# An attention and feed-forward kernel whose order of operations comes from deadlines: 141 recorded moves of the deadlines

## The chip, the cores and the metric

The kernel runs on one core of a Trainium2 chip. The metric is the time of one execution on the device in microseconds, from three runs of the kernel before. The engines are TensorE (PE; its weight loads are listed as PEld), VectorE (DVE), ScalarE (ACT), GpSimd (POOL) and SyncE (SP), which issues all transfers from and to memory.

## The reference

Attention of 8 batches and 8 heads, with keys and values averaged over 8 neighbours, and on its output a feed-forward layer of 512 to 2048 to 512 features:

```python
k_p = k.reshape(B, H, Sp, pool, D).mean(axis=3)          # B, H = 8, 8; S = 576, D = 64, pool = 8, Sp = 72
v_p = v.reshape(B, H, Sp, pool, D).mean(axis=3)
scores = scale * np.matmul(q, k_p.transpose(0, 1, 3, 2))
attn = softmax(scores)
x = np.matmul(attn, v_p) ...reshape(B * S, H * D)         # 4608 x 512
h = x @ w_in                                              # 512 x 2048
sp = np.maximum(h, 0.0) + np.log1p(np.exp(-np.abs(h)))
g = h * erf(sp)
return (g @ w_out).astype(np.float32)                     # 2048 x 512
```

## The kernel before

The 4608 tokens are nine chunks of 512. Attention makes the columns of x for a chunk (tiles att, in banks of PSUM): scores of up to 128 tokens (line 637), their maxima, differences, the exponential by way of a sigmoid, sums and scaling on VectorE, ScalarE and GpSimd (tiles m, s, z), transposes on TensorE (line 692), and the product with the values (lines 755, 756, 826). The feed-forward layer works on numbers that are split in a high and a low half, with three matmuls of 128x512 for each product (function `pairs`, line 826). A low half is the difference of line 446, which may run on VectorE or on GpSimd; a high half is line 434 (ScalarE) or 435 (GpSimd). Tiles h are the first GEMM, o the second, g the activated values between them, gl their halves; x and xr are the layer's inputs, w and ws weights and sums of weights.

Chunk 0 is computed plainly (stage 0). While this runs, the weights arrive in 64-bit words, are converted, and are written back to memory as halves. The other eight chunks go in pairs (stages 1 to 4), by a scheme with seven products instead of eight: function `quad` makes four tiles of h with seven products on four banks, and between the products VectorE adds what lies in a bank to a running sum (line 929). A second product onto a bank may start only when the addition that reads the first one is done. In stages 2 to 4 the second GEMM uses such a scheme too (function `seconds`, differences on line 992).

The activation of four tiles is two softplus operations of ScalarE for each pair (line 845), an error function for each pair (line 849), and a product on VectorE or GpSimd (lines 853, 856). Softplus and error function need different tables, and a change of table is an ACT_TABLE_LOAD. There are 8 banks of PSUM; a new tile waits until one is free.

Nothing of the order is written by hand. The kernel records operations with a deadline each, and the planner plays them through: method `once` starts, again and again, the operation that can start first on some engine, with costs per operation, limits on buffers and a price for a change of table, and its choice leans on the deadlines. Where an operation may run on two engines (`both`, `copy`, `out_of_bank`), `once` decides as well. The deadlines come from method `order`: eight passes, each with deadlines taken from the latest possible starts of the pass before; the best pass counts. Then the moves follow, of which the kernel before has none:

```python
for seed in MOVES:
    h = mix(seed)
    spread, reach = SPREAD[(h >> 20) % 3], REACH[(h >> 40) % 3]
    middle = -10000.0 + (mix(h ^ 0x1234567) >> 11) / 2.0 ** 53 * (SPAN + 10000.0)
    for i, t in enumerate(at):
        if abs(t - middle) < reach:
            g = mix(h + i)
            g = sum(float(g >> 16 * k & 65535) for k in range(4))
            at[i] = t + spread * ((g - 131070.0) / 37837.0)
```

Each seed stands for a middle, a reach (6, 20 or 60 us on the planner's scale) and a spread (0.3, 1 or 3 us): the deadlines within reach of the middle are shifted by random amounts. The operations are then played through once more with these deadlines, and written down in that order. Where the planner sees TensorE idle for over 1.2 us (in the first 57 us of its scale, for any time), it puts fillers into TensorE's queue, matmuls of constants onto the next free bank, 128x256 in bf16 (line 1127).

Of the kernel before, what the change touches and what calls it, by code (L numbers as in the profile page):

```python
# [41 lines left out]
BY_BLOCK = lambda ck: True  # L42
PASSES, UNIT = 8, 5100.0
SPREAD, REACH, SPAN = (300.0, 1000.0, 3000.0), (6e3, 20e3, 60e3), 860e3
MOVES = ()
T0, T0_STEP = -10.5, 1.5
VAL_R = 3.5
KEYS, KEYS_R, KEYS_S = -5.5, 0.5, -1.0
# [64 lines left out]
def mix(x):  # L113

    m = 2 ** 64 - 1
    x = x + 0x9E3779B97F4A7C15 & m
    x = (x ^ x >> 30) * 0xBF58476D1CE4E5B9 & m
    x = (x ^ x >> 27) * 0x94D049BB133111EB & m
    return x ^ x >> 31
# [33 lines left out]
class Program:  # L153
# [78 lines left out]
    def order(self, passes=PASSES):  # L232
# [13 lines left out]
        at = list(best[1])  # L246
        for seed in MOVES:
            h = mix(seed)
# [924 lines left out]
```

## Time and profile before

| | |
|---|---|
| time, median of 3 runs | 835.78 us (831.79 to 838.14) |
| the profiled execution's own time | 837.19 us |
| its span, first to last instruction | 835.4 us |
| mean granted clock of TensorE | 0.993 |
| TensorE busy | 811.6 us (97%) |
| VectorE, ScalarE, GpSimd busy | 696.5, 573.9, 445.2 us |
| read and written in memory | 167.84 and 49.28 MB |

Busy times are sums over the whole span, in which stages with different limits follow each other. Matmuls overlap in the record (one of 128x512 is listed with 381 ns), so that the time from one to the next is read from rows that hold many of them. The granted clock is the share of full speed that TensorE is given.

### The profile page before, as it was taken

Reading aid. Unit: us, or ns where it says so; the run is one execution under the profiler, and the core shown is the slowest. Engines: PE = TensorE matmul, PEld = TensorE weight load, DVE = VectorE, ACT = ScalarE, POOL = GpSimd, SP = SyncE. Lnnn points to the kernel's source line nnn. Section 1 sums busy time; section 2 is a strip of 40 time slices with the busy share of each in tenths; the row PEclk is TensorE's granted clock in tenths of the full one; section 3 lists DMA queues with packets and bytes.
Section 4 is the critical chain, followed back from the end, with each engine's and each line's share of the span. In section 5 each row is a group of like instructions: output and inputs, shape, how many; then the busy total and the mean of one; then the engine's idle time right before and its main releaser. Section 6 shows DMA issues by size and latency. Waiting matters only on the chain.

```text
span 835.4 us, 13512 instructions
## 1 busy us (share of the span) xinstructions
PE 811.6 (97%) x4091; PEld 703.4 (84%) x4091; DVE 696.5 (83%) x1235; ACT 573.9 (69%) x976; POOL 445.2 (53%) x441
## 2 busy tenths in 40 slices
PE   8998998999989989999999999999999999999998
PEld 7786887878878888888888888888878888888887
DVE  6976899887788999598988999978989995677972
ACT  5999876679974564477885544888955456999730
POOL 2884775568867871077657533363574311652330
PEclk9998999999999999999999999999999999999999
DMA  9889999799997899995486478943653689448641
GB/s 337 325 292 357 332 339 363 262 365 360 341 381 266 299 377 310 331 387 161 164 287 205 139 247 271 366 144 101 203 190 123 216 290 338 143 133 277 202 150 68
DMA packets 134695, 218.03 MB, mean 261 GB/s; under 512 B 17120, under 2 KB 49248, under 8 KB 134624
## 3 DMA queue, kind: packets, MB, share of 16 engines
q1 hardware_dynamic: 134624, 217.18, 75.6%
q8 instruction: 33, 0.54, 0.3%
q14 instruction: 38, 0.31, 0.1%
HBM read 167.84 MB, written 49.28 MB: 260 GB/s over the span
## 4 chain that ended last, share of the span: by engine, by line
PE 64%; DVE 6%; ACT 1%; issue 1%; DVEq 0%
PE o L826 31%; PE h L826 27%; PE att L637 3%; PE att L826 2%; PE att L692 1%; DVE s L684 1%; DVE gl L446 1%; PE att L756 1%; DVE e L708 1%; DVE vr L598 1%; DVE g L853 0%; DVE z L669 0%; ACT e L706 0%; DVE m L646 0%; ACT d L849 0%
## 5 line engine op out<-in xcount | busy, mean ns | idle before, releaser
L826 PE MATMUL o<-gl,w 128*128 128x512 f32 x1536 | 342.5, 381 | 4.7 <-DVE gl L446 4.2
L826 PEld LDWEIGHTS o<-gl,w 128*128 128x128 f32 x1536 | 287.2, 189 | 46.3 <-DVE gl L446 5.6
L826 PE MATMUL h<-x,w 128*128 128x512 f32 x1344 | 302.8, 385 | 3.9 <-DVE t L929 2.1
L826 PEld LDWEIGHTS h<-x,w 128*128 128x128 f32 x1344 | 255.4, 192 | 43.4 <-DVE t L929 3.0
L853 POOL TENSOR_TENSOR g<-d,g 128x512 f32<-128x512 f32 x76 | 98.9, 1318 | 132.6 <-ACT d L849 85.0
L434 ACT ACTIVATE gl<-g 128x512 fp32r<-128x512 f32 x177 | 102.7, 623 | 52.8 <-DVE g L992 27.5
L446 POOL TENSOR_TENSOR gl<-g,gl 128x512 fp32r<-128x512 f32 x63 | 90.7, 1445 | 77.9 <-ACT gl L434 73.4
L446 DVE TENSOR_TENSOR gl<-g,gl 128x512 fp32r<-128x512 f32 x145 | 114.3, 818 | 1.6 <-POOL gl L435 1.2
L929 DVE TENSOR_TENSOR g<-t,h 128x512 f32<-128x512 f32 x96 | 65.6, 685 | 27.8 <-PE h L826 26.7
L849 ACT ACTIVATE d<-d 128x1024 f32<-128x1024 f32 x72 | 74.1, 1053 | 0.5
L845 ACT ACT_TABLE_LOAD x48 | 61.6, 1283 | 14.5 <-PE h L826 13.2
L845 ACT ACTIVATE d<-g 128x512 f32<-128x512 f32 x103 | 59.1, 622 | 3.5 <-DVE g L929 3.4
L992 POOL TENSOR_TENSOR g<-g 128x512 f32<-128x512 f32 x40 | 53.4, 1338 | 11.5 <-DVE g L992 5.1
L849 ACT ACT_TABLE_LOAD x46 | 59.0, 1283 | 0.8
L929 DVE TENSOR_TENSOR t<-t,h 128x512 f32<-128x512 f32 x57 | 39.1, 686 | 22.1 <-PE h L826 18.1
L637 PE MATMUL att<-kbd,q 128*128 128x144 f32 (+1 forms) x320 | 46.8, 289 | 0.2 <-ACT kbd L587 0.2
L434 ACT ACTIVATE x<-xr 128x512 fp32r<-128x512 f32 (+2 forms) x53 | 28.7, 560 | 24.6 <-DVE xr L800 15.0
L637 PEld LDWEIGHTS att<-kbd,q 128*128 128x128 f32 (+1 forms) x320 | 41.6, 179 | 3.9 <-issue 0.7
L826 PE MATMUL h<-x,ws 128*128 128x512 f32 x192 | 44.1, 381 | 0.8 <-DVE x L446 0.5
L992 DVE TENSOR_TENSOR g<-g 128x512 f32<-128x512 f32 x56 | 42.9, 779 | 0.3
L646 DVE TENSOR_REDUCE m<-att 128x4 f32<-128x288 f32 (+1 forms) x80 | 34.3, 446 | 9.9 <-PE att L637 9.5
L826 PEld LDWEIGHTS h<-x,ws 128*128 128x128 f32 x192 | 35.9, 189 | 6.6 <-DVE x L446 0.9
(105 smaller groups left out, 1120.7 us busy)
## 6 DMA issues: line engine op xcount, KB each, us to landing
w<-ws SPq DMA_DIRECT2D x192, 256.0 KB, 4.8
w<-wo SPq DMA_DIRECT2D x136, 256.0 KB, 4.2
w<-wi SPq DMA_DIRECT2D x96, 256.0 KB, 5.1
ws<-ws SPq DMA_DIRECT2D x64, 256.0 KB, 4.7
v<-vl SPq DMA_DIRECT2D x48, 256.0 KB, 5.1
out<-f SPq DMA_DIRECT2D x35, 256.0 KB, 2.3
k<-kl SPq DMA_DIRECT2D x32, 256.0 KB, 5.2
q<-qa SPq DMA_DIRECT2D x32, 256.0 KB, 5.0
```

The costliest lines, as they stand in the source:

```text
L434: op("ACT", act(n), prio, lambda: nc.scalar.activation(dst(), src(), AF.Copy, scale=scale), *access, turn=turn, alt=("POOL", 0.833 * n + 1 ...
L446: both(True, dve(n), gps(n), prio + 0.1, lambda e: e.tensor_sub(lo(), src(), f32(hi())), reads + [hikey], [lokey])
L598: op("DVE", dve(4 * D), due + VALS_S, lambda mk=mk, sl=sl: nc.vector.scalar_tensor_tensor(vr.ap[:, :, sl], vs.ap[:, 0:NP, :], mk, f32(va.a ...
L637: nc.tensor.matmul(o, raw.ap[:, p, :T], kbd[:, p], start=(p % 2 == 0), stop=True, skip_group_check=True)
L646: op("DVE", dve(4 * SP), r + 0.4, lambda pv=pv, gs=gs: nc.vector.tensor_reduce(m.ap[:T, gs], pv(), AX.X, ALU.max), [ps], [(m, g)])
L684: both(ck < 3, dve(H * SP), gps(H * SP), r + 1.2, lambda e: e.tensor_mul(*[s.keys[:T].rearrange("t p (x k) -> t p x k", x=2)] * 2, z.ap[:T ...
L826: nc.tensor.matmul(o, u, v, start=first and q == 0, stop=last and q == 2, skip_group_check=True)
L845: nc.scalar.activation(y(k), hs[k][0].ap, AF.Softplus)
L849: op("ACT", act(1024), prio + 0.2, lambda k=k: nc.scalar.activation(ys[k].ap, ys[k].ap, AF.Erf), own[2 * k:2 * k + 2], own[2 * k:2 * k + 2 ...
L853: both(True, dve(512), gps(512), prio + 0.3, lambda e, k=k, h=h: e.tensor_mul(h.ap, y(k), h.ap), [own[k], h], [h])
L929: op("DVE", dve(512), prio, lambda: nc.vector.tensor_add(dst.ap, u.ap, o.ap), [u, o], [dst])
L992: both(True, dve(512), gps(512), prio, lambda e: e.tensor_sub(out.ap, u.ap, v.ap), [u, v], [out])
```

## The change

The table `MOVES` is filled with 141 seeds. They were found by a local search that played the whole order through for each trial. Nothing else is changed; lines below the table move by 13, so that line 826 is 839 in the changed kernel, 929 is 942, 446 is 459, 853 is 866.

```diff
-MOVES = ()
+MOVES = (
+    2000003, 2000010, 2000013, 2000026, 2000038, 2000052, 2000055, 2000062, 2000073, 2000099, 2000108,
...
+    2300967, 2328338, 2374855, 2378219, 2382978, 2438662, 2462926, 2495042,)
```

All five engines get another order. TensorE has 3876 rows before and 3812 after (180 fillers with a weight load each before, 148 after), VectorE 1216 and 1214, ScalarE 890 and 913, GpSimd 446 and 441, SyncE 815 both times. Table loads of ScalarE are 97 before and 87 after. Three places follow.

The first place is VectorE in stage 1, where the products of the quads meet the first matmuls of the second GEMM (some 226 to 235 us of the trace before). Tiles t are running sums of a quad, h its banks. Before:

```order
L929 TENSOR_TENSOR t_3006<-t_3000,h_2973 128x512
L446 TENSOR_TENSOR ws_3017<-sw_2921,ws_2986 128x512
L853 TENSOR_TENSOR g_2877<-d_2954,g_2877 128x512
L853 TENSOR_TENSOR g_2835<-d_2939,g_2835 128x512
L853 TENSOR_TENSOR g_2717<-d_2874,g_2717 128x512
L446 TENSOR_TENSOR gl_3045<-g_2472,gl_2997 128x512
L929 TENSOR_TENSOR t_3058<-t_3006,h_3034 128x512
L578 TENSOR_REDUCE vs_2925<-v_3003 128x64
L929 TENSOR_TENSOR g_3074<-t_3058,h_3049 128x512
L929 TENSOR_TENSOR g_3085<-t_3006,h_3034 128x512
```

And now, at the same place:

```order
L942 TENSOR_TENSOR t_2999<-t_2984,h_2976 128x512
L675 TENSOR_TENSOR s1_72<-att_2895,m_2965 128x2x144
L866 TENSOR_TENSOR g_2855<-d_2929,g_2855 128x512
L866 TENSOR_TENSOR g_2794<-d_2949,g_2794 128x512
L866 TENSOR_TENSOR g_2732<-d_2840,g_2732 128x512
L459 TENSOR_TENSOR gl_3043<-g_2333,gl_3025 128x512
L459 TENSOR_TENSOR gl_3056<-g_2562,gl_3036 128x512
L942 TENSOR_TENSOR t_3063<-t_2999,h_3029 128x512
L591 TENSOR_REDUCE vs_2917<-v_3011 128x64
L591 TENSOR_REDUCE vs_2917<-v_3058 128x64
L942 TENSOR_TENSOR g_3088<-t_3063,h_3049 128x512
L942 TENSOR_TENSOR g_3101<-t_2999,h_3029 128x512
```

Between the two additions into t there now stand two low halves (gl) instead of one and a difference of a softmax tile (s1) instead of a difference of weights (ws); the three products (g) stay. The same place on TensorE, from the last matmul of the first product onto the bank h_3034 to the first of the second. Before:

```order
L826 MATMUL h_3034<-x_2238,ws_3017 128x512
L826 MATMUL h_3049<-x_2108,ws_2952 128x512
L826 MATMUL h_3049<-x_2134,ws_2952 128x512
L826 MATMUL h_3049<-x_2108,ws_2969 128x512
L826 MATMUL h_3049<-x_2119,ws_2952 128x512
L826 MATMUL h_3049<-x_2140,ws_2952 128x512
L826 MATMUL h_3049<-x_2119,ws_2969 128x512
L826 MATMUL h_3034<-x_2288,w_2756 128x512
```

Now the bank is h_3029; the last six matmuls onto it stand seven to twelve rows ahead of this piece's third row:

```order
L839 MATMUL h_3049<-x_2147,ws_2903 128x512
L839 MATMUL h_3049<-x_2129,ws_2921 128x512
L839 MATMUL h_3049<-x_2118,ws_2903 128x512
L839 MATMUL h_3049<-x_2135,ws_2903 128x512
L839 MATMUL h_3049<-x_2118,ws_2921 128x512
L839 MATMUL o_2990<-gl_2608,w_3027 128x512
L839 MATMUL o_2990<-gl_2852,w_3027 128x512
L839 MATMUL o_2990<-gl_2608,w_3027 128x512
L839 MATMUL o_2994<-gl_2608,w_3027 128x512
L839 MATMUL o_2994<-gl_2852,w_3027 128x512
L839 MATMUL o_2994<-gl_2608,w_3027 128x512
L839 MATMUL h_3029<-x_2293,w_2821 128x512
```

Where six matmuls onto another bank stood between the two products, there are now these and six of the second GEMM.

The second place is ScalarE at the end of stage 0 (some 85 to 95 us of the trace before). Tiles d hold softplus and then its error function, cv, w0 and xr are other work. Before:

```order
L845 ACT_TABLE_LOAD
L845 ACTIVATE d_1230<-h_1121 128x512
L845 ACTIVATE d_1230<-h_1155 128x512
L849 ACT_TABLE_LOAD
L849 ACTIVATE d_1230<-d_1230 128x1024
L495 ACTIVATE cv_1262<-d_1143 128x512
L495 ACTIVATE cv_1275<-d_1153 128x512
L495 ACTIVATE cv_1279<-d_1173 128x512
L434 ACTIVATE w0_1289<-f0_1277 128x512
L440 COPY xr_1300<-att_1286 128x64
L667 ACTIVATE s3_74<-s3_74,cst_75 128x4x144
L845 ACT_TABLE_LOAD
```

And now:

```order
L858 ACT_TABLE_LOAD
L858 ACTIVATE d_1280<-h_1189 128x512
L858 ACTIVATE d_1280<-h_1123 128x512
L858 ACTIVATE d_1295<-h_1216 128x512
L858 ACTIVATE d_1295<-h_1251 128x512
L862 ACT_TABLE_LOAD
L862 ACTIVATE d_1280<-d_1280 128x1024
L862 ACTIVATE d_1295<-d_1295 128x1024
L608 ACTIVATE va_1359<-vs_520,cst_75 128x4x64 x2
```

Two pairs of softplus operations stand together, and then both error functions: two table loads for four tiles, where two tiles had two.

The third place is late in stage 1, where the second chunk's output begins (some 291 to 297 us of the trace before). There VectorE had, with gl_3842 the low half that the seventh group of matmuls onto the new banks uses:

```order
L446 TENSOR_TENSOR ws_3788<-sw_3675,ws_3742 128x512
L578 TENSOR_REDUCE vs_3800<-v_3181 128x64
L578 TENSOR_REDUCE vs_3800<-v_3231 128x64
L578 TENSOR_REDUCE vs_3800<-v_3255 128x64
L669 TENSOR_REDUCE z_3830<-s1_72 128x8
L674 RECIPROCAL z_3830<-z_3830 128x8
L446 TENSOR_TENSOR gl_3842<-g_2497,gl_3685 128x512
L578 TENSOR_REDUCE vs_3800<-v_3828 128x64
```

In the new order this half is gl_3791, on GpSimd:

```order
L554 TENSOR_TENSOR sw_3518<-sw_3518,sw_3491 128x256
L555 TENSOR_TENSOR sw_3722<-sw_3606 128x256
L556 TENSOR_TENSOR sw_3583<-sw_3482,sw_3518 128x256
L459 TENSOR_TENSOR ws_3741<-sw_3518,ws_3724 128x512
L459 TENSOR_TENSOR ws_3758<-sw_3583,ws_3743 128x512
L553 TENSOR_TENSOR sw_3776<-sw_3606,sw_3548 128x256
L459 TENSOR_TENSOR gl_3791<-g_2499,gl_3683 128x512
L554 TENSOR_TENSOR sw_3776<-sw_3776,sw_3606 128x256
L459 TENSOR_TENSOR gl_3822<-g_2475,gl_3701 128x512
```

The half has moved from VectorE, where sums of values (vs) and of a softmax tile (z) stood ahead, to GpSimd, where sums and differences of weights (sw, ws) stand ahead.

## Rows read from the trace of the kernel before

**Rows 1.** The page, part 1: busy us (share of the span) x instructions.

```profile
PE 811.6 (97%) x4091; PEld 703.4 (84%) x4091; DVE 696.5 (83%) x1235; ACT 573.9 (69%) x976; POOL 445.2 (53%) x441
```

**Rows 2.** The chain that ended last, 300 to 360 us: start, us, what.

```profile
317.64 25.90 PE o L826 x120
```

**Rows 3.** By stretch: busy us of PE, PEld, DVE, ACT, POOL; granted clock; DMA share, GB/s.

```profile
36.00:93.00 57.00, 53.26 (x254) 45.73 (x252) 41.05 (x77) 53.69 (x70) 39.98 (x45) 0.94 0.96 325
93.00:187.00 94.00, 90.10 (x455) 76.19 (x454) 84.39 (x146) 68.17 (x127) 61.70 (x71) 1.00 0.93 331
...
245.00:300.00 55.00, 52.84 (x283) 46.11 (x282) 49.39 (x98) 30.67 (x64) 45.46 (x49) 1.00 0.90 304
300.00:598.00 298.00, 296.85 (x1520) 260.85 (x1519) 263.44 (x492) 201.13 (x335) 149.31 (x138) 1.00 0.72 245
598.00:630.00 32.00, 29.56 (x155) 25.30 (x154) 28.89 (x56) 19.78 (x43) 19.87 (x20) 1.00 0.55 181
```

**Rows 4.** TensorE's waits: us in total, times, longest.

```profile
PE o L826 <- DVE gl L446: 4.2, 3, 2.2
PE att L1127 <- DMA cst<-cst: 2.7, 1, 2.7
PE att L692 <- DVE g L856: 2.3, 1, 2.3
...
PE h L826 <- DVE t L929: 2.1, 1, 2.1
```

**Rows 5.** TensorE's timeline at 204 us: start, us, line, tiles, count [idle before].

```profile
203.85 1.37 PE L1127 MATMUL h<-cst 128*128 128x256 bf16 x11
...
206.37 2.03 PE L1127 MATMUL h<-cst 128*128 128x256 bf16 x17
```

**Rows 6.** Busy us in two short stretches, columns as in rows 3.

```profile
66.00:74.00 8.00, 7.15 (x21) 5.58 (x20) 4.79 (x9) 7.63 (x12) 4.10 (x5) 0.57 1.04 343
233.00:238.00 5.00, 4.18 (x12) 3.44 (x13) 3.17 (x7) 0.91 (x2) 2.71 (x4) 0.66 1.05 396
```

**Rows 7.** Timeline at 62 to 68 us, ScalarE and TensorE.

```profile
63.81 2.00 ACT L849 ACTIVATE d<-d 128x1024 f32<-128x1024 f32 x2
...
65.73 0.43 PE L692 MATMUL att<-cst,s 64*128 64x64 f32 x4 [2.27 <-DVE g L856]
...
67.29 7.99 PE L826 MATMUL h<-x,w 128*128 128x512 f32 x22 [0.32 <-DVE g L856]
```

**Rows 8.** Timeline at 227 to 234 us, VectorE and TensorE.

```profile
227.01 4.49 DVE L853 TENSOR_TENSOR g<-d,g 128x512 f32<-128x512 f32 x3
...
231.42 1.75 DVE L446 TENSOR_TENSOR gl<-g,gl 128x512 fp32r<-128x512 f32 x1
...
233.82 4.51 PE L826 MATMUL h<-x,w 128*128 128x512 f32 x12 [2.11 <-DVE t L929]
```

**Rows 9.** ScalarE's timeline at 58 us: a table load and what follows.

```profile
58.28 1.28 ACT L845 ACT_TABLE_LOAD   x1
...
59.57 1.09 ACT L845 ACTIVATE d<-h 128x512 f32<-128x512 f32 x2
```

**Rows 10.** TensorE's waits from 75 to 125 us.

```profile
PE h L826 <- DVE g L856: 0.6, 1, 0.6
PE o L826 <- DVE g L856: 0.4, 1, 0.4
```

**Rows 11.** TensorE's timeline at 294 to 298 us.

```profile
296.31 1.99 PE L826 MATMUL o<-gl,w 128*128 128x512 f32 x8 [2.16 <-DVE gl L446]
```

**Rows 12.** The page, part 5: low halves on GpSimd and on VectorE.

```profile
L446 POOL TENSOR_TENSOR gl<-g,gl 128x512 fp32r<-128x512 f32 x63 | 90.7, 1445 | 77.9 <-ACT gl L434 73.4
L446 DVE TENSOR_TENSOR gl<-g,gl 128x512 fp32r<-128x512 f32 x145 | 114.3, 818 | 1.6 <-POOL gl L435 1.2
```

**Rows 13.** Timeline at 617 to 627 us, TensorE.

```profile
618.74 0.63 PE L692 MATMUL att<-cst,s 128*128 128x128 f32 x4 [1.03 <-DVE s L684]
...
627.05 3.29 PE L826 MATMUL o<-gl,w 128*128 128x512 f32 x14 [1.32 <-DVE gl L446]
```

11 rows, old and new, of the table MOVES are left out of this document.

## Prediction

> **What bounds the kernel now.** I read first the busy shares, then the stretches, then TensorE's waits, then the timeline at the longest of them. The busy shares name TensorE: 811.6 us of 835.4 [rows 1]. How long that work must take at the least is better seen in a stretch without any wait: 120 matmuls of 512 columns took 25.90 us there [rows 2], 0.216 us each, and nearly every matmul of the kernel is of this form. The stretches [rows 3] show where more than that is lost. From 300 to 598 us TensorE is busy 296.85 of 298 us: no order can win anything there. What can be won lies before 300 us, and a little at 598 to 630 us, and there other engines are close to their own limit: ScalarE with 53.69 of 57 us from 36 on, VectorE with 84.39 of 94 us from 93 on. TensorE's waits after the start add up to little: the three large groups behind the first transfer are 8.6 us [rows 4], all others some 8 us more. To these come 37 fillers after the start (matmuls without use that the planner sets where it expects a gap; two groups stand in [rows 5], 28 of the 37), and two stretches in which the granted clock falls, 0.57 on the mean from 66 to 74 us and 0.66 from 233 to 238 us [rows 6], to the lower of the two levels (1.2 GHz), each just behind a wait of TensorE of over 2 us. At that level 22 matmuls took 7.99 us [rows 7] where 22 x 0.216 = 4.75 us would do, a loss of 3.2 us; 12 matmuls took 4.51 us [rows 8] against 2.6, a loss of 1.9 us. So the whole that an order can win behind the start is about 17 (waits) + 37 x 0.11 = 4.1 (fillers) + 5.1 (clock) = 26 us.
>
> The sum is made against the profiled execution, 837.19 us, of which 835.4 are the span; the median of the three runs, 835.78, is 1.4 us below it, and the result is moved down by that.
>
> **The change, part by part.** No operation is added or taken away from the computation. What changes is the order on all five engines, on which of two engines an operation runs where the planner may choose, the number of table loads, and the number of fillers.
>
> Fillers. One of them is 0.11 us: 17 took 2.03 us and 11 took 1.37 us, six more in 0.66 us [rows 5]. Before there are 143 ahead of the first useful matmul of the first GEMM and 37 behind it; now 138 and 10. The ten stand in one group early in the same stage, and the groups of 11, 17 and 9 are gone. A filler stands in TensorE's queue and is always executed, so each one less is a gain if its gap is gone too: 32 x 0.11 = 3.5 us. If the gap stays and only its cover goes, the gain is nothing. I take all of it, since what stood around the two large groups was moved as well (next paragraphs).
>
> Table loads of ScalarE. Each takes 1.28 us [rows 9], and there are 97 before, 87 now. Up to the 16th softplus 14 become 12, up to the 32nd 26 become 22, because four softplus operations now more often stand together and then their two error functions. In the first of these stretches that is 2 x 1.28 = 2.6 us off an engine that is busy 94% of it. But TensorE follows ScalarE there at a few places only: its waits for a bank that a product of softplus and error function must free are 0.6 and 0.4 us [rows 10], and 2.27 us at 65.7 us [rows 7]. This last one I leave as it is: ScalarE's two error functions for four banks [rows 7] stand in the same place of the changed order, with one operation of 0.6 to 1 us less ahead of them. So of 2.6 us I count 1.0; the bounds are 0 and 2.6. In the Trainium skill, "ScalarE: Activation LUTs", section "What ACT_TABLE_LOAD costs", a switch is said to cost a load and a drain, some 2.66 us together. The next activation here starts 1.29 us after a load began [rows 9], so that no drain shows behind it; by the page the two loads would be 5.3 us and the sum lower by up to 2.7 us.
>
> The wait at 231.7 us. In a quad (four tiles made by seven products) the second product onto a bank must wait until VectorE has added up the first. Before, six matmuls (1.3 us) lie between the two, and VectorE had three products of 1.5 us each, a subtraction of 1.75 us and the addition ahead [rows 8]; TensorE stood still for 2.11 us, and the clock fell. Now twelve matmuls lie between (1.3 us more cover). VectorE's work between the two additions concerned is about the same: three products, two subtractions instead of one and a small one of a softmax tile, no weight difference. So the wait should fall from 2.1 to about 0.8 us, and a wait of that length stood nowhere before a drop in these rows: 1.3 + 1.9 = 3.2 us. Bounds: 0 if VectorE is as much later as TensorE, and 4.0.
>
> The wait at 294.2 us. TensorE waited 2.16 us for the low half of an operand, which VectorE made as the last of a chain without idle time [rows 11]. At the corresponding place of the new order GpSimd makes it, behind a row of weight sums. A half takes 1.445 us there and 0.818 on VectorE [rows 12]; GpSimd was busy 45.46 of 55 us in this stretch [rows 3], so it is not free either. I count half, 1.1 us; bounds -1 (GpSimd is later still) and 2.2. A rule of the Trainium skill speaks against this move ("SBUF — State Buffer", section "Who interferes with whom"): an operation of VectorE with both inputs in SBUF and one of GpSimd that reads SBUF exclude each other through a shared port. Rows agree as far as they go: VectorE's products took 1.5 us each beside a busy GpSimd [rows 8]. By it the halves moved would take back what they give, and this term would be 0.
>
> The waits at 617 and 625 us, 1.03 and 1.32 us [rows 13]. The first is for the scaling of a softmax tile. Now the two transposes that follow the last scores are those of tiles scaled long before (VectorE's rows 922 and 941, the last maxima being rows 955 and 956), and the remaining two stand behind 54 more matmuls, 11.7 us. The second wait is for a half on VectorE, which is as full as before (28.89 of 32 us). I count the first alone: 1.0; bounds 0 and 2.4.
>
> The start and the end are left: the same 45 fillers, and the last 339 matmuls stand as before. Loads from memory are reordered too (815 rows of SyncE both times); the one wait of TensorE for a transfer is the first, 2.7 us [rows 4], and I price this at nothing; a weight that comes late would cost up to such a wait, and one that comes earlier gains nothing, as none is waited for.
>
> The sum: 3.5 + 1.0 + 3.2 + 1.1 + 1.0 = 9.8 us. 837.2 - 9.8 = 827.4, less 1.4: **826 us**, 1.2% below the median.
>
> **Rivals.** (a) The waits move and don't go. VectorE is busy 88 to 90% in the four stretches shown from 93 us on [rows 3], so what is taken from one wait comes back at the next; only fillers count, and about 32 x 0.11: 835.8 - 3.5 = 832 us. For it: each of the shown waits hangs on a different instruction, and all of them are reordered. Against it: ScalarE's ten loads less and the longer distance in the quads are real relief. (b) The new order is slower. From 93 to 187 us VectorE is busy 90%. In the new order 328 of its rows lie ahead of the 32nd addition of the quads, before 322; at 696.5 us / 1235 = 0.56 us [rows 1] that is 3.4 us, and if VectorE is the bound there, TensorE waits for them in two or three pieces of over 2 us (together with what is waited there now). Each can bring a drop as behind 65.7 us: 3.4 + 3 x 3.2 - 3.5 = +9.5 us, 845 us. It decides if such a wait is over 2 us long. Against it: TensorE's waits in this stretch are short now, and of the three long ones (2.27, 2.11, 2.16 us) one had no drop behind it. (c) Almost all waits go: 835.8 - 26 = 810 us. For it: the planner sees fewer gaps of the size that it fills, one where there were three; against it: a wait at 65.7 us whose order did not change.
>
> **How the numbers follow.** Forecast 0.45, (a) 0.29, (b) 0.16, (c) 0.10. The forecast's own range is made of its bounds: all terms at their best 3.5 + 2.6 + 4.0 + 2.2 + 2.4 = 14.7 us (821), at their worst only part of the fillers and one late half, about 833. Some 1% (8.4 us) is what a measurement of this kernel can tell from no change, since its three runs are 6 us apart. 826 is just outside of it, so that about a fifth of the forecast's chance lies within: faster 0.36 + 0.10 = 0.46, within 1% 0.09 + 0.29 = 0.38, slower 0.16. The range from 813 to 841 us takes in the forecast, (a), half of (c) and little of (b).
>
> **What would show it.** In the profile after: TensorE's busy time down by some 3.5 us with 148 rows of the filler; 43 and 42 table loads at the two lines of the activation where 48 and 46 were; no wait of TensorE over 1 us, and no granted clock under 0.9, where the quads of the first stage meet the second GEMM (some 225 to 240 us); the wait at 65.7 us and the drop behind it still there. The prediction is wrong if the clock falls at a new place before 250 us, if VectorE's additions of the quads release TensorE more often than before, or if TensorE waits for a transfer.

## The result and the profile after

The changed kernel takes 824.09 us (median of 4 runs, 822.35 to 824.77), the kernel before 835.70 us beside it (4 runs, 831.79 to 838.14): ratio 0.9862, interval 0.9821 to 0.9903. The forecast was 826 us. Over all 81 executions of the kernel before that were made beside the experiments its median is 836.66 us. The profiled execution of the changed kernel took 822.35 us, span 820.5 us, with a mean granted clock of 1.000. Against the profiled execution of before that is 14.9 us of span, more than the medians show (11.6). Both are single executions, and that of before has two drops of the clock (mean granted clock 0.993, where the 81 have 0.989 to 0.999).

The page of the changed kernel, part 1, as in [rows 1]:

```profile
PE 801.7 (98%) x4059; PEld 697.5 (85%) x4059; DVE 695.4 (85%) x1224; ACT 568.9 (69%) x982; POOL 446.6 (54%) x436
```

Its stretches, columns as in [rows 3]:

```profile
36.00:93.00 57.00, 54.99 (x274) 47.13 (x273) 45.20 (x83) 54.92 (x74) 45.63 (x51) 1.00 0.94 331
93.00:187.00 94.00, 89.88 (x461) 77.53 (x460) 84.50 (x149) 70.25 (x130) 56.39 (x63) 1.00 1.00 353
187.00:245.00 58.00, 58.00 (x282) 50.56 (x281) 53.81 (x86) 52.96 (x67) 45.84 (x45) 1.00 0.99 350
245.00:300.00 55.00, 54.17 (x303) 47.67 (x302) 49.46 (x97) 31.75 (x75) 39.02 (x45) 1.00 0.90 317
```

The kernel before in the one of these stretches that [rows 3] leave out:

```profile
187.00:245.00 58.00, 55.89 (x270) 47.92 (x269) 44.62 (x69) 51.90 (x63) 44.80 (x44) 0.97 1.02 358
```

The clock is 1.00 in all four stretches, its upper level. TensorE stands still nowhere from 187 to 245 us, and VectorE does 53.81 us of work there where it did 44.62, although its work over the whole span is the same (695.4 and 696.5 us). TensorE's longest waits, as in [rows 4] (line 705 is 692 in the kernel before, 768 is 755):

```profile
PE att L705 <- DVE s L697: 3.0, 4, 1.3
PE att L1140 <- DMA cst<-cst: 2.6, 1, 2.6
PE att L768 <- DVE s L675: 2.2, 1, 2.2
PE h L839 <- DVE t L942: 1.6, 2, 0.9
PE att L708 <- POOL bb L693: 1.4, 1, 1.4
PE att L705 <- DVE g L869: 1.1, 1, 1.1
```

Of the three waits of over 2 us that the kernel before has behind the start none is left; one of 2.2 us, at 120 us, is new. The waits for low halves are down from 4.2 us to 0.2. Around 62 to 66 us, as in [rows 7]:

```profile
61.93 2.01 ACT L862 ACTIVATE d<-d 128x1024 f32<-128x1024 f32 x2
...
63.77 0.24 PE L708 MATMUL att<-cst,bb 64*64 64x64 f32 x1 [0.20 <-DVE g L869]
...
65.09 0.46 PE L705 MATMUL att<-cst,s 64*128 64x64 f32 x4 [1.09 <-DVE g L869]
...
65.78 8.01 PE L839 MATMUL h<-x,w 128*128 128x512 f32 x36 [0.23 <-DVE g L869]
```

ScalarE's two error functions begin 1.9 us earlier than before, TensorE waits 1.5 us in three pieces, and 36 matmuls behind them take 8.01 us (0.22 each), where before 22 took 7.99. At the quads, as in [rows 8]:

```profile
226.07 1.46 PE L839 MATMUL o<-gl,w 128*128 128x512 f32 x6
226.39 0.68 DVE L942 TENSOR_TENSOR t<-t,h 128x512 f32<-128x512 f32 x1
...
227.36 2.75 PE L839 MATMUL h<-x,w 128*128 128x512 f32 x12
```

VectorE's addition ends at 227.07, 0.29 us ahead of the second product. Table loads are 43 and 42, as the order said, 1.283 us each:

```profile
L858 ACT ACT_TABLE_LOAD x43 | 55.2, 1283 | 22.7 <-PE h L839 12.7
...
L862 ACT ACT_TABLE_LOAD x42 | 53.9, 1283 | 0.7
```

Since waits move, where the time went is best read from TensorE's own progress: when it starts its 1st, 140th, 460th, 930th and last (3133rd) matmul of 512 columns. The starts were counted in the traces; the table gives the time between them in us, for both kernels and five of the experiments below (each is one profiled execution).

| | to 1st | to 140th | to 460th | to 930th | to last |
|---|---|---|---|---|---|
| before | 36.3 | 38.1 | 95.6 | 127.2 | 533.5 |
| changed | 35.7 | 34.2 | 95.7 | 117.9 | 532.3 |
| e5: moves of deadlines under 110 us | 36.1 | 34.3 | 95.2 | 129.2 | 534.6 |
| e6: moves from 110 us | 35.8 | 37.7 | 104.7 | 117.9 | 530.9 |
| e7: moves under 330 us | 36.3 | 34.2 | 97.7 | 118.1 | 533.9 |
| e8: moves from 330 us | 36.3 | 36.4 | 95.2 | 129.1 | 534.8 |
| e4: before with four edits by hand | 35.7 | 37.3 | 95.7 | 122.3 | 536.2 |

Nearly all of the gain lies in two pieces: 3.9 us up to the 140th matmul (about 70 us), and 9.2 us between the 460th and the 930th (166 to 284 us). The second piece can be added up from the two traces: before, it holds 28 fillers (3.0 us), 5.1 us of TensorE's waits and the drop behind the wait at 231.7 us (1.9 us, as the prediction reckoned it); in the changed kernel it holds no filler, 1.4 us of waits and no drop. That is 8.6 of the 9.2 us. The experiments ask what made all three go.

### The profile page after: what moved, and what is told of

Same layout as the page of the kernel before. It is cut to its first block, busy times and chain, and to the rows that moved or that the text cites. A ratio compares the mean times of both kernels' runs of the same rounds, so it can differ in the third digit from the quotient of the medians.

```text
span 820.5 us, 13391 instructions
## 1 busy us (share of the span) xinstructions
PE 801.7 (98%) x4059; PEld 697.5 (85%) x4059; DVE 695.4 (85%) x1224; ACT 568.9 (69%) x982; POOL 446.6 (54%) x436
## 4 chain that ended last, share of the span: by engine, by line
PE 47%; DVE 2%; DMA 1%; ACT 0%; issue 0%; DVEq 0%; SPq 0%; ACTq 0%
PE o L839 24%; PE h L839 19%; PE att L650 1%; PE att L839 1%; PE att L705 1%; DVE g L1005 1%; DVE gl L459 1%; DMA w<-ws 1%; DVE s L697 0%; PE att L769 0%; PE att L708 0%; ACT gl L447 0%; DVE etb L737 0%; DVE e L721 0%; ACT e L719 0%
## 5 line engine op out<-in xcount | busy, mean ns | idle before, releaser
L839 PE MATMUL h<-x,w 128*128 128x512 f32 x1344 | 297.5, 380 | 2.3 <-DVE t L942 1.6
L839 PEld LDWEIGHTS h<-x,w 128*128 128x128 f32 x1344 | 252.4, 189 | 39.6 <-DVE t L942 2.4
L459 DVE TENSOR_TENSOR gl<-g,gl 128x512 fp32r<-128x512 f32 x149 | 116.8, 815 | 1.8 <-POOL gl L448 0.9
L459 POOL TENSOR_TENSOR gl<-g,gl 128x512 fp32r<-128x512 f32 x59 | 85.5, 1454 | 53.4 <-ACT gl L447 52.6
L459 DVE TENSOR_TENSOR x<-xr,x 128x512 fp32r<-128x512 f32 (+2 forms) x55 | 38.1, 714 | 1.6 <-ACT x L447 1.6
```

The lines of the kernel that those rows point to most:

```text
L459: both(True, dve(n), gps(n), prio + 0.1, lambda e: e.tensor_sub(lo(), src(), f32(hi())), reads + [hikey], [lokey])
L839: nc.tensor.matmul(o, u, v, start=first and q == 0, stop=last and q == 2, skip_group_check=True)
```

## The experiments

The first four kernels are the kernel before with edits of the finished list of operations, behind the line that makes it. They test the theory of the prediction: each wait hangs on a few instructions, and with these moved it goes and the time is kept. The kernels were timed in three groups (e1 to e4, e5 to e8, e9 to e12) with the kernel before beside each; its medians are 836.68, 836.36 and 837.34 us, and 835.70 beside the changed kernel, so that differences of 1 or 2 us between groups are not firm. The ratio on record is not the quotient of the two medians, and where they differ both are used.

**e1, no fillers behind 57 us.**

```diff
     ops = pr.order()
+    ops = [o for i, o in enumerate(ops) if i < 400 or not isinstance(o, tuple)]
```

> The kernel before without its 37 fillers behind the first 57 us; the order of every operation stays. Local theory (the prediction's term): the gaps they were set for are not there, so TensorE gains 37 x 0.11 = 4.1 us, about 831.6 us against 835.7. Rival (VectorE and ScalarE set the pace there): TensorE waits as long as the fillers ran, 835 to 836 us. A third: fillers hold the clock up, and without them it falls near 204 or 517 us, which would cost some 2 to 3 us each and show in the granted clock.

Measured: 837.12 us (12 runs) against 836.68 (35 runs), ratio 1.0001 (0.9983 to 1.0019). TensorE's timeline where the second of the two groups stood:

```profile
207.79 2.43 PE L826 MATMUL h<-x,ws 128*128 128x512 f32 x10 [1.32 <-DVE ws L446]
```

The gaps were there: 1.32 us at 206 us and 0.51 at 213, for 28 fillers (3.0 us). So of the fillers' time more than half is a wait for VectorE. In this one profile the span is 2.7 us shorter than in the profile of before, but the median does not move. Nor do the 2.7 us lie at the fillers: at the 660th matmul of 512 columns (218 us) TensorE is no further than before, and it gains 2.7 us up to the 750th, where its wait for the running sum (t), 2.11 us in [rows 8], is 1.04 us with no drop behind it:

```profile
232.75 2.86 PE L826 MATMUL h<-x,w 128*128 128x512 f32 x12 [1.04 <-DVE t L929]
```

The granted clock is 0.994 on the mean of the 12 runs, against 0.996 for before; where that is lost the one profile does not show, so the third case stays open.

**e2, one conversion from ScalarE to GpSimd.**

```diff
+    ops[446].fn = ops[446].choice["POOL"][1]
```

> The kernel before with one conversion (tile low, 0.99 us, at 60.55 us) taken from ScalarE to GpSimd, four rows ahead of the two error functions that TensorE waits for at 65.7 us. ScalarE has no idle time from 43 us to there. Theory that ScalarE's queue sets this wait: it falls from 2.27 to about 1.3 us, and if the drop of the clock behind it hangs on a wait of over 2 us, the drop goes too (3.2 us): 4.2 us in all, about 831.5 us. If the drop does not hang on the wait's length: 1.0 us, about 834.7 us. Rival (GpSimd, with 0.98 us more, is late for a low half and the wait comes back): 835 to 836 us.

Measured: 837.09 us, ratio 1.0017 (0.9999 to 1.0034). The error functions did start 1.07 us earlier (62.74), but the wait grew. VectorE and TensorE at 60 to 67 us:

```profile
61.40 0.69 DVE L446 TENSOR_TENSOR w<-f,w 128x512 fp32r<-128x512 f32 x1 [2.86 <-POOL w L435]
63.42 0.69 DVE L446 TENSOR_TENSOR w<-f,w 128x512 fp32r<-128x512 f32 x1 [1.33 <-POOL w L435]
...
66.28 0.65 PE L692 MATMUL att<-cst,s 64*128 64x64 f32 x4 [2.92 <-DVE g L856]
```

The conversion went in ahead of the second of two halves of weights on GpSimd; VectorE stands at the differences that need these halves, and the product that frees TensorE's bank is behind them in its queue. In the kernel before this product waited only 0.26 us for ScalarE:

```profile
64.90 0.69 DVE L856 TENSOR_TENSOR g<-d,h 128x512 f32<-128x512 f32 x1 [0.26 <-ACT d L849]
```

So two queues end together at this place, and the edit shortened one and lengthened the other. The rival was right here, by weights instead of a low half.

**e3, an addition of the quad two places up.**

```diff
+    ops.insert(1364, ops.pop(1371))
```

> The kernel before with one addition of a quad (tile t, at 233.09 us) moved up two places on VectorE, ahead of the third product and the low half. Nothing else changes. Local theory: TensorE's wait of 2.11 us at 231.7 us and the drop of the clock behind it (1.9 us) go: 4.0 us, about 831.7 us. Rival: the product and the half, 0.7 us later each, make TensorE wait a few us further on for as long; 834 to 836 us, with the drop of the clock gone or moved.

Measured: 835.31 us, ratio 0.9983 (0.9962 to 1.0004). At its place the edit did all that was expected: no wait of TensorE for a running sum (t) is left, and the clock stays up. But behind the wait at 291 us (2.2 us, as in before) the clock now fell, which it does not in the profile of before. Two stretches, columns as above:

```profile
228.00:242.00 14.00, 13.63 (x69) 11.43 (x68) 14.00 (x19) 13.45 (x17) 11.53 (x12) 1.00 1.01 352
290.00:302.00 12.00, 9.83 (x45) 8.28 (x44) 10.00 (x17) 5.75 (x12) 5.68 (x6) 0.86 1.04 373
```

So 3.4 us were gained from 228 to 241 us, and 1.7 us of them lost by 313 us to a drop of the clock (TensorE's progress against before). Over 12 runs 1.4 us are left, and the interval takes in none at all.

**e4, four edits together.** The three above, and at 294 us one low half up:

```diff
+    ops.insert(1718, ops.pop(1725))
```

> The kernel before with four edits by hand in place of the 141 moves: no fillers behind 57 us, the conversion on GpSimd, the addition two places up, and at 294 us the low half ahead of the sum and the reciprocal of a softmax tile (0.95 us). Local theory: the gains add, 4.1 + 4.2 + 4.0 + 0.9 = 13.2 us, about 822.5 us, as much as the changed kernel has (824.1). Rival (what is taken from one wait comes back at the next, and only another order throughout gives the gain): 830 to 834 us.

Measured: 833.20 us, ratio 0.9960 (0.9943 to 0.9977): 3.5 us, a quarter of the sum. By the table e4 takes 4.9 us of the 9.2 between the 460th and the 930th matmul, only 0.8 us up to the 140th (the misplaced conversion), and a new wait later takes back some of it:

```profile
658.98 3.29 PE L826 MATMUL o<-gl,w 128*128 128x512 f32 x14 [1.58 <-POOL gl L446]
```

The theory as it stood has fallen: a wait is not the property of one instruction. The theory that replaced it: the gain lies in how VectorE's work is spread over whole stretches, and within a stretch it does not need the rest of the order. The next four kernels test this. They are the changed kernel, with the moves in force for a part of the deadlines only:

```diff
+        at = [a if -1e9 <= t < 110e3 else t for a, t in zip(at, best[1])]
         for prios in ([t / UNIT for t in at], best[2]):
```

**e5 to e8.** The bounds are as shown for e5, from 110 us on for e6, under 330 us for e7, from 330 us on for e8.

> The changed kernel, but only deadlines under 110 us (on the planner's scale) are moved; later ones stay as in the kernel before. The list of operations is the changed kernel's for its first 612 entries (to about 90 us), then one of its own. In the changed kernel's profile TensorE is 4.7 us ahead of before at that place, the wait at 65.7 us being shorter and the clock not falling behind it. Theory that leads add up, place by place: 4.7 us are kept to the end, about 832 us against 836.7. Rival (a lead is eaten by the next waits, since VectorE and ScalarE are as full as before): 835 to 837 us, and the lead against before is under 2 us at 300 us.

> The complement: only deadlines from 110 us on are moved; the first 608 entries of the list are those of the kernel before. Leads that add up: 12.6 us of the whole change less the 4.7 us of the first stretch, about 829 us. Rival (the later moves fit only to the start that they were found with): 833 us or more.

> Only deadlines under 330 us are moved; the list is the changed kernel's for its first 1881 entries (to about 310 us). There the changed kernel is 12.7 us ahead in the profiles, of 14.9 us at the end. Leads that add up: 12.7/14.9 of 12.6 us, some 10.7 us, about 826 us. Rival (the lead is eaten in the untouched rest, where TensorE's waits fall on VectorE again): 829 us or more.

> Only deadlines from 330 us on are moved; the first 1873 entries are those of the kernel before. Leads that add up: 2.2/14.9 of 12.6 us, some 1.9 us, about 835 us, not to be told from before. Rival (the late moves bring most of the gain): 831 us or less.

Measured, against 836.36 us (29 runs):

| | us | ratio (interval) |
|---|---|---|
| e5, under 110 | 834.17 | 0.9968 (0.9948 to 0.9987) |
| e6, from 110 | 834.89 | 0.9969 (0.9950 to 0.9987) |
| e7, under 330 | 826.74 | 0.9868 (0.9842 to 0.9893) |
| e8, from 330 | 836.27 | 0.9987 (0.9970 to 1.0003) |

The cut at 330 us adds up: e7 and e8 together have 9.7 us by the medians and 12.1 by the ratios, against 11.6 for the whole, and nearly all of it is earned before the cut. The cut at 110 us does not: 2.2 and 1.5 us by the medians, 2.7 and 2.6 by the ratios. e5 lies between its two forecasts, and its lead at 300 us, 1.5 us in the profile, is that of its rival; e6 is where its rival was. The table says why. Between the 460th and the 930th matmul e6 needs 117.9 us, as the changed kernel does (117.9) and e7 (118.1), while e5, e8 and before need 127 to 129. So these moves bring their 9 us after either start. Between the 140th and the 460th, though, e6 loses 9 us, to a wait of a length that neither of the two full orders has (the changed kernel waits 2.17 us for the same line):

```profile
125.82 1.30 PE L651 MATMUL att<-kbd,q 128*128 128x144 f32 x4 [6.26 <-DVE s L676]
126.75 7.03 PE L840 MATMUL o<-gl,w 128*128 128x512 f32 x24
```

A wait of 6.26 us, and 24 matmuls at 0.29 us behind it. Of e5's lead at the 140th matmul (4.1 us by the profile of before, 2.4 and 3.1 by those of e8 and e6, which begin as before does) its median shows 2.2 us.

What goes with the 9 us is seen at VectorE. In the 62 us from the 460th matmul on (170 to 232 us before, 165 to 227 in the changed kernel), VectorE's waits, with the lines of before and then of the changed kernel:

```profile
DVE g L929 <- PE h L826: 5.7, 10, 0.7
DVE t L929 <- PE h L826: 4.5, 9, 0.6
```

```profile
DVE g L942 <- PE h L839: 5.2, 8, 1.1
DVE t L942 <- PE h L839: 1.8, 3, 0.6
```

Before, VectorE stands 19 times for a product of TensorE that is not done yet, 10.2 us together, with low halves and products of the activation queued behind; at 231 and 294 us TensorE waits for an addition behind such work, and for a half. Now it is 11 times and 7.0 us, and other work stands between the additions: of the additions in these 62 us, 23 before and 17 now follow right on the one ahead. VectorE is busy 54.6 of the 62 us there (e7 54.3, e6 52.3), against 49.4 before (e5 49.8, e8 49.7, e4 49.2). Where the order of the quads is the old one, VectorE does 2 to 5 us less, whatever else is edited. The fillers are not what holds it up: without them, in e1, it is busy 50.1 us.

That VectorE's order is the cause of the 9 us, and not only goes with it, is argued and not shown: e5 to e8 move all five engines' orders together, and no run has the new order of one engine alone. By edits of the old order e4 brings 4.9 of the 9.2 us, and undoing one piece of TensorE's new order (e11, below) costs 1.4.

**e9, both queues ahead of 65.7 us,** in the kernel before:

```diff
+    ops.insert(449, ops.pop(456))
+    o = ops.pop(446)
+    o.fn = o.choice["POOL"][1]
+    ops.insert(457, o)
```

> The kernel before with both queues shortened ahead of the wait at 65.7 us: the conversion (tile low) goes from ScalarE to GpSimd, this time behind the two halves of weights (w) that VectorE waits for, and VectorE's low half (gl, 0.68 us) goes ahead of its two differences of weights, into an idle stretch of 2.8 us. Theory that two queues end there within 0.3 us of each other: the wait falls from 2.27 to about 1.4 us and no drop of the clock follows; 0.9 us and up to 3.2 us for the drop, about 833 us against 836.5. Rival (the wait hangs on neither, or GpSimd is late again): still over 2 us with a drop, 836 us or more.

Measured: 834.93 us against 837.34 (17 runs), ratio 0.9975 (0.9958 to 0.9993): 2.4 us. TensorE at 65 us, and the clock behind it:

```profile
65.20 0.43 PE L692 MATMUL att<-cst,s 64*128 64x64 f32 x4 [1.72 <-DVE g L856]
```

```profile
66.00:74.00 8.00, 7.45 (x27) 6.17 (x28) 4.71 (x10) 7.83 (x11) 4.15 (x5) 0.79 1.00 334
```

The wait shrinks by 0.55 us, and not by some 0.9: the half that was moved up ran beside GpSimd and took 1.76 us instead of 0.68. The drop is shorter, not gone. The time lies between the two forecasts. With both queues shortened the gain is there, with one of them (e2) it is not. But e2 also put the conversion at another place on GpSimd, and VectorE's edit alone was not run, so that the need for both is likely and not shown.

**e10, ScalarE later in the changed kernel.**

```diff
+    ops[447:447] = [ops[446]] * 3
```

> The changed kernel with one copy on ScalarE (0.62 us, at 59.97 us) done three times more, 1.9 us ahead of the two error functions that TensorE waits for at 63.8 to 65.8 us. Theory that ScalarE's load up to here is what the lead at this place hangs on: the waits grow from 1.5 to about 3.4 us, the clock falls behind them (2 to 3 us), and the lead of 3.9 us against before is gone there; about 824 + 1.9 + 2.5 = 828.5 us. Rival (what is lost here is regained, since TensorE's next waits, at 113 and 120 us, are for VectorE and shrink as TensorE comes later): 824 to 826 us.

Measured: 826.35 us (6 runs, 825.07 to 829.21), ratio to before 0.9877 (0.9849 to 0.9906). The changed kernel, which was not timed beside it, has 0.9862; its four runs (822.35 to 824.77) lie below all six. TensorE's timeline:

```profile
65.17 0.24 PE L708 MATMUL att<-cst,bb 64*64 64x64 f32 x1 [2.26 <-DVE g L869]
66.50 0.46 PE L705 MATMUL att<-cst,s 64*128 64x64 f32 x4 [1.08 <-DVE g L869]
```

The wait is back, a drop stands behind it (0.79 from 64 to 72 us), and at the 140th matmul 3.1 us of the lead are gone. The medians differ by 2.3 us: less than the first theory said (4.4), and close to the rival's 824 to 826 us. In the profile 3.1 us are still missing at the last matmul, but a second drop is in it (0.86 from 120 to 132 us), behind the 2.18-us wait that has none in the changed kernel; what that drop cost was regained elsewhere, among other places at 168 us, where a wait of 0.89 us is gone.

**e11, the six matmuls of cover taken from the quad,** in the changed kernel:

```diff
+    ops.insert(1367, ops.pop(1362))
```

> The changed kernel with six matmuls of the second GEMM (at 226.07 us) moved behind the product that follows them, so that they no longer stand between the two products onto a bank of a quad: the prediction's term of 3.2 us, undone. In the changed kernel's profile VectorE's addition ends 0.29 us ahead of the second product. Theory (distance is what took the wait away): a wait of about 1.0 us comes back, no drop behind it as it is under 2 us; about 825 us. If the prediction's term was right in size: about 827 us, with the granted clock under 0.9 there. Rival (VectorE's order took the wait away): no wait, 824 us.

Measured: 825.49 us, ratio to before 0.9866 (0.9839 to 0.9892). TensorE's timeline:

```profile
228.15 1.56 PE L839 MATMUL h<-x,w 128*128 128x512 f32 x6 [0.90 <-DVE t L942]
```

The wait comes back with 0.90 us, no drop behind it. So the distance is worth about 1 us; the rest of what was won here has another source, and VectorE being less far behind is the likely one.

**e12, the changed kernel improved by hand,** by VectorE's order alone:

```diff
+    ops.insert(3300, ops.pop(3303))
+    ops.insert(2538, ops.pop(2549))
+    ops.insert(1083, ops.pop(1075))
+    for k, i in enumerate((775, 777, 779, 783)):
+        ops.insert(769 + k, ops.pop(i))
+    w, g = ops.pop(735), ops.pop(732)
+    ops[745:745] = [g, w]
```

> The changed kernel with its own waits taken on by hand, by places in VectorE's order alone: at 120 us the maxima and differences of a softmax tile ahead of two low halves (2.17 us), at 113 us two sums (etb) ahead of a low half and a weight (0.79), at 167 us a difference of weights behind the quad's addition (0.7), at 449 and 614 us the scaling of a softmax tile ahead of sums of g (1.29 and 1.21). Theory (a wait goes where what is moved back is not needed soon, as a look at its readers shows): 6.2 us at most, some 819 us. Rival (the waits come back, as with the four edits of the kernel before, which gave a quarter): 822 to 823 us.

Measured: 821.54 us (5 runs, 820.87 to 822.30), ratio to before 0.9812 (0.9786 to 0.9838); all five runs are below the four of the changed kernel. So 2.5 us of 6.2, between the two forecasts. None of the five waits is longer than 0.63 us now. But those at 120 and 449 us have a successor a little later, the second for a half behind the scaling that was moved up:

```profile
135.62 0.70 PE L839 MATMUL o<-gl,w 128*128 128x512 f32 x2 [0.65 <-DVE w L459]
```

```profile
454.28 1.99 PE L839 MATMUL o<-gl,w 128*128 128x512 f32 x8 [1.38 <-DVE gl L459]
```

In the profiles e12 is only 0.7 us ahead of the changed kernel. The granted clock is 0.998 to 1.000 in all five runs, against 0.996 to 1.000 in the four of the changed kernel; how much of the 2.5 us is the 2.2-us wait that can no longer be followed by a drop was not measured by itself.

## Why the prediction was right, and where it was not

The direction and the size were right (826 for 824.09), by terms of which some were too high and one, put at nothing, was worth some 2 to 4 us. That these nearly cancel is luck; the sum's 9.8 us stand against 11.6 by the medians and 14.9 by the two profiles. By its own steps:

- *Fillers, 3.5 us.* 148 rows, as the order said. As a price for each filler the term is wrong: with the fillers alone taken out (e1) nothing is gained, as VectorE's gap is under them. It holds only because the gap went as well, which came with the new order of the quads (e6 and e7 have no filler there, e5 and e8 have all 28).
- *Table loads, 1.0 us, and the wait at 65.7 us left as it is.* This is the step that failed. The wait fell from 2.27 to 1.5 us in three pieces, and the drop behind it is gone: 3.9 us up to the 140th matmul in the profiles, some 2 to 3 us in medians (e5, e10). I had compared the few operations just ahead of the error functions and not ScalarE's whole queue, which runs there without a gap: from 35 to 63 us five conversions (low, some 0.95 us each) stood on ScalarE, and now two (GpSimd has seven instead of five). e10 shows that the lead is lost when ScalarE gets more to do; e2 and e9 speak for VectorE and GpSimd having to come earlier too. What the two table loads saved give by themselves was not measured.
- *The wait at 231.7 us, 3.2 us.* Gone with its drop; TensorE needs 2.7 us less from the 660th to the 750th matmul (218 to 243 us before). The reason given, the distance of twelve matmuls, is worth 0.9 to 1.4 us (e11). That VectorE's work ahead was "about the same" was true of the rows between the two additions, and not of the 60 us ahead of them.
- *The wait at 294.2 us, 1.1 us.* It is gone, the half is on GpSimd and in time. What this is worth by itself was not tried: attention's matmuls stand elsewhere now, and the progress does not tell them apart. On the rule of the shared port that spoke against the move, see the last section: a half on VectorE costs more beside a busy GpSimd, before as after, and in the kernel before the 22 halves of GpSimd that overlapped VectorE's (line 446) by over 30% of their time took 1.69 us on the mean, 73 others 1.33.
- *The waits at 617 and 625 us, 1.0 us.* The wrong one went: the scaling of a softmax tile is still waited for (1.21 us at 615 us), the low half is not.
- *Start, end and transfers, 0.* Right: TensorE waits for one transfer, the first, 2.6 us.

Of what would show it, TensorE's busy time fell by 9.9 us and not 3.5, since besides the fillers matmuls at the lower clock are listed as longer (640 ns on the mean from 67 to 73 us before, 379 in the changed kernel); the clock from 225 to 240 us is 1.00 with no wait, as forecast; the wait at 65.7 us with its drop was forecast to stay and did not. One of the signs of being wrong did come: TensorE waits for additions of the quads (t and g) three times, 1.8 us together, where before it was twice, 2.4 us. They are more often, at 168, 183 and 402 us, but shorter.

Rival (a), waits that move and don't go, holds for single edits (e1 to e4: 3.5 of 13.2 us) and for e12, and not for the change: it rests on VectorE being full in the four stretches that I showed, while in the one I left out, 187 to 245 us, it had 13.4 us to spare, most of it in line for TensorE. Of rival (b), a new wait of over 2 us with a drop, the changed kernel has the wait, at 120 us, and its profile no drop; e7 has the same wait with a drop behind it, and e6 the worst form of it.

## What to carry to other kernels

Where two engines take turns waiting for each other, look first for idle time of the second engine ahead of the waits of the first: VectorE stood idle for 12.6 of the 62 us ahead of the wait at 231 us, and for 7.4 in the new order, where this wait and the one at 294 us are gone; the shift of a single instruction (e3) left 1.4 us of the 4.0 expected, and the interval takes in none. Here this is what goes together, not a proof that the one pays for the other. Before an instruction is moved off a busy queue, ask which other queue ends within half a microsecond of it, and what stands behind the new place. A part of a set of moves that was found by playing the whole order through may keep its gain, and lose as much at the place where it meets an order that it was not found with (e6).

## What the runs showed of the hardware

**VectorE beside GpSimd.** Here, in the kernel before, are 182 low halves and differences on VectorE with two inputs in SBUF (L446, 128x512; the 43 of x are left out), and the 163 additions of the quads, which read a bank of PSUM (L929), sorted by how much of their time GpSimd was in an operation of its own (those in between are not shown):

```
                 GpSimd free (under 5%)   GpSimd busy (over 60%)
L446, SBUF+SBUF  113 x 681 ns             55 x 1144 ns (670 to 2154)
L929, SBUF+PSUM   49 x 686 ns            102 x  685 ns
```

The changed kernel shows the same (123 x 680 and 55 x 1149 ns), so that the moves gained little by it. One row of it, 128x256, beside two low halves on GpSimd (the other five of its kind took 0.41 to 0.69 us):

```profile
108.81 3.08 DVE L615 TENSOR_TENSOR vm<-vs,cst 128x256 f32<-128x256 f32 x1
...
109.09 2.52 POOL L459 TENSOR_TENSOR gl<-g,gl 128x512 fp32r<-128x512 f32 x2
```

The Trainium skill ("SBUF — State Buffer", section "Who interferes with whom") calls it an exclusive lock for an operation with two inputs in SBUF, and none for one with a single input there; these rows agree with both halves of the rule.

**The drop of the clock is not certain.** The wait of 2.17 us at 120 us has no drop behind it in the changed kernel (1.00 from 120 to 130 us), and one in e7 behind a wait of the same 2.17 us (0.83 is a mean over time at the upper and at the lower level):

```profile
120.00:130.00 10.00, 7.83 (x30) 6.32 (x29) 9.97 (x16) 4.98 (x9) 5.98 (x6) 0.83 1.01 356
```

The four kernels with this wait are split: the changed kernel and e11 without a drop, e7 and e10 with one. In e9 a drop stands behind a wait of 1.72 us at 65 us, and none behind its waits of 2.10 and 2.15 us at 233 and 294 us, so the length of the wait alone does not decide. Executions of one kernel differ too: of 81 of the kernel before, the two with a mean granted clock of 0.999 took 831.9 and 832.1 us, the twelve with 0.993 a median of 837.6 us. The changed kernel has one such wait where before has three, and its four runs are 2.4 us apart, against 6.4 us for the four of before beside them.
